# Opening durations re-entered in a build-time planner, and key-value products over five sets of positions

## The chip, the cores and the metric

The kernel runs on one core of one Trainium2 chip. The metric is the device time of one execution in microseconds (us); the time given for a kernel is the median of several executions.

## What is computed

Eight batches with eight heads of linear attention (576 positions, head width 64) are followed by a mixture of four two-layer networks ("experts") over all 4608 positions. Everything is float32.

```python
kv  = einsum('bhsd,bhse->bhde', k, v)          # q, k, v: (8, 8, 576, 64)
o   = einsum('bhsd,bhde->bhse', q, kv)
rms = sqrt(mean(o * o, axis=-1, keepdims=True) + 1e-6)
x   = (o / rms * g_norm).transpose(0, 2, 1, 3).reshape(4608, 512)
p   = domain_probs / (domain_probs.sum(-1, keepdims=True) + 1e-9)   # (4608, 4)
out = sum over e of p[:, e:e+1] * (relu(x @ w1[e]) @ w2[e])         # w1: 512x1024, w2: 1024x512
```

## The kernel before

**Tiling.** The 4608 positions are cut into nine chunks of 512: of each batch the first 512 positions make a chunk (c = 0 to 7), and the eight remainders of 64 positions together make the ninth. A stage is one expert on one chunk, s = 9·e + c, 36 in all. In a stage, up makes the hidden activations and down or down_deep the output; both are fast matrix products with seven products in place of eight, some at two levels, whose sums and differences of blocks run on VectorE (DVE) and GpSimd (POOL). The first stage alone uses up_plain (L999), plain products of 512 columns. During expert 0 the attention of batch c+1 is interleaved with stage c.

**Attention of one batch.** Heads are handled in four pairs (hp). load_pair brings q (two DMAs of 128 KB per pair), k and v (288 KB each; 96 partitions, on each six neighbouring positions of 64 values for each of two heads) in. For each pair: the PE transposes q (turn, L651), ScalarE (ACT) copies it to SBUF (L656); the PE multiplies k by v over six sets of 96 positions, two heads each (key_values, L665), ACT copies the result (L678); the PE multiplies q by it (attend, L691) into two PSUM tiles "raw". Then scaled: ACT squares them (L564), DVE sums (L571), POOL raises to the power -1/2 (L578, L582), DVE multiplies (L591), which is the last reader of raw. At the end the PE transposes the result (turn_x, L709) and ACT stores it as a half of x with the gain (L717). Batch 0 does this pair by pair; the others join two pairs into one group, so that one key_values has 24 products. Raw is in the PSUM banks "db" and "u2" for batch 0 in alternation, in "db" for batch 1, and in "ab" after that. The banks "db" also take the products of down (L1126). The remainder of each batch goes through turn_rem, attend_rem and turn_xrem (L735, L753, L769).

**Who sets the order.** Every operation is put into a Plan with a key (its wanted place), a duration per engine that it may run on, and its buffers. Plan.layout runs a list schedule once, when the kernel is built: it goes through time, gives each engine the next operation that its model calls ready, assigns buffers and PSUM banks, and so fixes the order of instructions on each engine. On the chip the engines keep that order and wait for each other by semaphores; the modelled times have no other effect. The PE and the DMA-issuing queue of SyncE (SP) take the first ready operation in order of keys, the others the most urgent. A load's end is modelled by one shared bus: `bus = max(bus, t + 1.5) + op.kb / 215.0`, plus 0.5, with at most eight loads on their way.

**Idle work.** While the next key on the PE is below 0 (that is, before the first product of up_plain in the ordinary order) and the model has nothing ready for the PE, it puts two transposes of the identity into a free PSUM bank (idle, L1353), which keep the PE running. In the model such a pair lasts:

```python
op = Op(front, {"PE": 0.23}, None, (), (), 0, False)
op.start, op.eng, op.end = t, eng, t + 0.23
```

weights_1 loads the four quarters of an expert's first matrix (512 KB each) and makes its sums, weights_2 the second. x_forms makes the sums of x for a stage. All sums go through combine (L360). norm_probs loads and normalizes p.

Of the kernel before, what the change touches and what calls it, by code (L numbers as in the profile page):

```python
# [34 lines left out]
class Plan:  # L35
# [13 lines left out]

    SPARE = {"big": 6, "small": 3}  # L50
    STEP, LATE = 44.0, 20.0

    def __init__(self):
        self.ops = []
# [26 lines left out]
    def layout(self, slots, later, idle, idle_banks, idle_until):  # L81
# [20 lines left out]
                cross = self.SAME if op.cost.keys() == d.cost.keys() else self.CROSS  # L102
                d.due = min(d.due, op.due - cross - min(d.cost.values()))
        busy = {e: 0.0 for e in todo}
        bus, port = 3.0, 0.0
        lanes = [0.0] * self.LANES
        t = 0.0
        wake = [0.0, 1.6]
# [24 lines left out]
        while left:  # L133
# [4 lines left out]
            for eng in todo:  # L138
# [25 lines left out]
                if best is not None:  # L164
                    op = best
# [38 lines left out]
                if eng == "PE" and busy[eng] <= t and 1.6 <= t and front < idle_until:  # L204
                    kind, spare = next((
                        (k, f) for k in idle_banks for f in free[k] if f[0] <= t
                    ), (None, None))
                    if spare is not None:
                        op = Op(front, {"PE": 0.23}, None, (), (), 0, False)
                        op.start, op.eng, op.end = t, eng, t + 0.23  # L210
                        op.fn = lambda eng, bank=slots[kind][spare[1]]: idle(bank)
                        busy[eng] = op.end
                        free[kind].remove(spare)
                        free[kind].append((op.end, spare[1]))
                        heapq.heappush(wake, op.end)
                        order.append(op)
                        moved = True
# [13 lines left out]
def kernel(  # L231
# [36 lines left out]
    nc = tc.nc  # L268
# [8 lines left out]
    NCH = B + 1  # L277
    HN = NT // 2
    HF = F // 2
    KR = 6  # L280
    KP = S // KR
    EPS = 1e-6
    NBLK = NCH * NR
    assert H * D == DM == NT and D == 64 and P == 128 and NPAIR == 4 and F == 1024
    assert REM == D and REM * B == NT and KP * KR == S and KP <= P

    const = ctx.enter_context(tc.tile_pool(name="const", bufs=1))
    pool = ctx.enter_context(tc.tile_pool(name="pool", bufs=1))
# [120 lines left out]
    def w1_src(e, dh, uh):  # L409
        rows = moe_w1[e][dh * 2 * P:(dh + 1) * 2 * P, uh * HF:(uh + 1) * HF]  # L410
        return rows.rearrange("(kt p) f -> p kt f", p=P)
# [19 lines left out]
    def weights_1(e, key, step, need):  # L431

        f = {n: Buf("big", f"w1_{e}_{n}") for n in (1, 2, 21, 4, 5, 6, 7, 3)}
        corner = {}
        w1corner[e] = {}
        for i, (n, dh, uh) in enumerate(((1, 0, 0), (2, 1, 0), (21, 0, 1), (4, 1, 1))):
            corner[n] = Buf(None, f"w1c_{e}_{n}")
            w1corner[e][uh, dh] = f[n], corner[n]
            load(
                key + i * step, f[n],  # L440
                lambda n=n: f[n].ap[:].rearrange("p (k u) -> p k u", k=2),
                w1_src(e, dh, uh), 512, also=[corner[n]],
            )

        def form(k_, o, a, b, op):
            corner[o] = Buf(None, f"w1c_{e}_{o}")
            combine(
                k_, either(1024), lambda: f[o].ap[:], lambda: f[a].ap[:], lambda: f[b].ap[:], op,
                [f[a], f[b], corner[a], corner[b]], [f[o], corner[o]],
            )  # L450

        def from_dram(k_, o, a, dh, uh):
            corner[o] = Buf(None, f"w1c_{e}_{o}")
            subtract_from(
                k_, f[o], lambda ap: ap[:].rearrange("p (k u) -> p k u", k=2), f[a],
                w1_src(e, dh, uh), [f[a], corner[a]], [f[o], corner[o]],
            )

        def sums():
            form(need + 0.25, 5, 21, 4, ALU.add)  # L460
            form(need + 0.26, 6, 5, 1, ALU.subtract)
            if e:
                from_dram(need + 0.5, 7, 21, 0, 0)
                from_dram(need + 0.5, 3, 6, 1, 0)
            else:
                form(need + 0.5, 7, 1, 21, ALU.subtract)
                form(need + 0.5, 3, 2, 6, ALU.subtract)
            w1f[e] = {}
            for j, m in enumerate(OUTER):
                x, low, y = f[m], corner[m], Buf("w1y", f"w1y_{e}_{m}")  # L470
                parts = {}
                for n, (uq, kt) in ((1, (0, 0)), (2, (0, 1)), (7, (1, 0)), (4, (1, 1))):
                    parts[n] = (
                        [x, low] if n == 7 else [x],
                        lambda x=x, uq=uq, kt=kt: two(x.ap[:])[:, kt, uq * HN:(uq + 1) * HN],
                    )
                for n, at in ((5, 0), (6, 1), (3, 2)):
                    parts[n] = ([y], lambda y=y, at=at: y.ap[:, at * HN:(at + 1) * HN])
                for o, a, b, op in (
                    (5, 7, 4, ALU.add), (7, 1, 7, ALU.subtract), (6, 5, 1, ALU.subtract),  # L480
                    (3, 2, 6, ALU.subtract),
                ):
                    combine(
                        need + j / 7, either(HN), parts[o][1], parts[a][1], parts[b][1], op,
                        parts[a][0] + parts[b][0], [low] if o == 7 else [y],
                    )
                w1f[e][m] = parts

        return sums
# [111 lines left out]
    def attention(b, key, span, rem):  # L601
# [6 lines left out]
        at = lambda j: key + span * j / (NPAIR + 1)  # L608
        qTs, kvs = {}, {}

        def load_pair(hp):
            hs = slice(2 * hp, 2 * hp + 2)
            n = f"{b}_{hp}"
            kind = "kv" if b or hp < 2 else "big"
            kt, vt, qt = Buf(kind, f"k{n}"), Buf(kind, f"v{n}"), Buf("small", f"q{n}")
            want = at(hp) - 0.25 if b else key - 1 + 0.1 * hp
            for r in range(2):
                load(
                    want, qt,
                    lambda qt=qt, r=r: qt.ap[:].rearrange(  # L620
                        "p (r h d) -> p r h d", h=2, d=D)[:, :, r, :],
                    q[b, 2 * hp + r, 0:NT, :].rearrange("(p r) d -> p r d", r=NR), 128,
                )
            for t, src in ((kt, k), (vt, v)):
                load(
                    want, t,
                    lambda t=t: t.ap[0:KP, 0:2 * KR * D].rearrange("p (h x) -> p h x", h=2),
                    src[b, hs].rearrange("h (p j) d -> p h (j d)", j=KR), 288,
                )
            return kt, vt, qt  # L630

        def kv_rows(t):
            return t.ap[0:KP, 0:2 * KR * D].rearrange("p (h j d) -> p h j d", h=2, d=D)

        groups = ((0,), (1,), (2,), (3,)) if b == 0 else ((0, 1), (2, 3))
        for g, pairs in enumerate(groups):
# [4 lines left out]
            for o, hp in enumerate(pairs):  # L641
# [6 lines left out]
                def turn(eng, bank=bank, qt=qt):  # L648
                    for r in range(NR):
                        rs = slice(r * P, (r + 1) * P)  # L650
                        nc.tensor.transpose(bank.ap[:, rs], qt.ap[:, rs], ident[:])  # L651

                plan.add(at(hp), pe(4, P, 1), turn, reads=[qt], writes=[bank])
                plan.add(
                    at(hp), act(NT),
                    lambda eng, bank=bank, qT=qT: nc.scalar.activation(  # L656
# [3 lines left out]

            def key_values(eng, bank=kbank, held=held):
                for o, (kt, vt) in enumerate(held):
                    for j in range(KR):
                        for r in range(2):
                            nc.tensor.matmul(  # L665
                                bank.ap[r * D:(r + 1) * D, o * D:(o + 1) * D],
                                lhsT=kv_rows(kt)[:, r, j, :], rhs=kv_rows(vt)[:, r, j, :],
                                start=(j == 0), stop=(j == KR - 1), skip_group_check=True,
                            )

            size = len(pairs)
            plan.add(
                at(pairs[-1]), {"PE": 0.73 * size + 0.2}, key_values,
                reads=[t for ts in held for t in ts], writes=[kbank],
            )
            plan.add(
# [2 lines left out]
                    out=to.ap[:, 0:size * D], in_=bank.ap[:, 0:size * D], func=ACT.Copy),  # L679
                reads=[kbank], writes=[kv],  # L680
            )
            raw = [Buf(("db", "u2")[r] if b == 0 else "ab" if b > 1 else "db", f"raw{n}_{r}") for r in range(2)]

            def attend(eng, raw=raw, kv=kv, pairs=pairs):
                for o, hp in enumerate(pairs):
# [300 lines left out]
    def up_plain(s, e, c, key, span):  # L986
# [4 lines left out]
        for i in range(8):  # L991
            uh, a, u = i // 4, i // 2 % 2, i % 2
            bank = Buf("u1" if a == 0 else "u2", f"up{s}_{i}")
            for dh in range(2):
                w, low = corners[uh, dh]

                def product(eng, w=w, bank=bank, dh=dh, ut=2 * a + u):
# [5 lines left out]
                        )  # L1003

                op = plan.add(
                    key + span * i / 8 - (1.1 if i < 2 and dh == 0 else 0.0), pe(2, NT), product,
                    reads=[w, low, xh[dh]], **({"parts": [bank]} if dh else {"writes": [bank]}),
                )
                op.marks = bank, NT
# [297 lines left out]

    plan.add(-2.85, {"SP": 1.1}, load_gains, writes=[gains], kb=1)
    attention(0, -2.0, 1.3, 0.1)
    sums_1 = weights_1(0, -2.5, 0.02, 0.3)  # L1310
    up_plain(0, 0, 0, 0.0, 1.0)
    sums_1()
    x_forms(0, 0.3)
    x_views = {}
    inner = {0: weights_2(0, 0.25, 0.02, 7.6)}
    norm_probs(0.3)
    for e in range(E):
        for c in range(NCH):
            s = e * NCH + c
            if e == 0 and c + 1 < B:  # L1320
                attention(c + 1, s - 0.1, 0.8, s + 0.5)
            if e + 1 < E and c == NCH - 1:
                weights_1(e + 1, s + 0.0, 0.12, s + 0.4)()
                inner[e + 1] = weights_2(e + 1, s + 1.0, 0.13, s + 1.55)
            if s + 1 < E * NCH:
                if e == 0 and c + 1 < NCH:
                    x_views[s + 1] = x_forms(c + 1, s + 0.7)
# [76 lines left out]
```

## Time and profile before

| | |
|---|---|
| median of 9 runs | 1723.47 us (1723.13 to 1723.83) |
| the profiled execution | 1723.22 us, of which 1721.4 us is the span from its first to its last instruction |
| mean granted TensorE clock | 0.999 |
| DVE busy | 1235.1 us (72%) |
| ACT busy | 974.6 us (57%) |
| POOL busy | 677.6 us (39%) |
| DMA moved | 230.42 MB, mean 134 GB/s |

The page gives the busy time of each engine, the span in 40 slices, the DMA queues, the chain of work that ended last, and groups of instructions. PE is the matmul stream, PEld the loading of weights beside it, SPq the issue of DMAs. A float32 product is two records in the trace, a transpose one. The heaviest groups on the PE are the products of up:

```profile
L912 PE MATMUL u<-xf,big 128*128 128x128 f32 x3104 | 452.4, 275 | 0.0
L912 PE MATMUL u<-xf,w1y 128*128 128x128 f32 x2652 | 390.9, 275 | 0.0
```

The columns are line, engine, operation, tiles, shapes and count, then busy us, mean ns of one, and idle time ahead.

### The profile page before, as it was taken

What the parts mean: (1) busy time and instruction counts of PE and PEld (TensorE: products, weight loads), DVE (VectorE), ACT (ScalarE), POOL (GpSimd) and SP (SyncE); (2) the same over time, 40 slices, a digit from 0 to 9 for tenths busy, and PEclk for the clock granted to TensorE, in tenths of its full rate; (3) what the DMA queues carried; (4) which work ended last, traced back from release to release, by engine and by line L of the source; (5) the groups of instructions that cost most, each with busy time, mean ns of one, the idle gap of its engine ahead of it and who ended that gap; (6) DMA issues with size and microseconds to landing.
All of it is one profiled execution on the core that took longest, in us unless ns stands there. A gap on an engine that the chain in (4) does not pass through costs nothing.

```text
span 1721.4 us, 39248 instructions
## 1 busy us (share of the span) xinstructions
PE 1711.9 (99%) x15586; PEld 1653.0 (96%) x15586; DVE 1235.1 (72%) x2034; ACT 974.6 (57%) x2378; POOL 677.6 (39%) x613
## 2 busy tenths in 40 slices
PE   9999999999999999999999999999999999999998
PEld 7699999999999999999999999999999999999998
DVE  4755655565777777777788787777788787777774
ACT  3354544454455665565666566666666666656562
POOL 3421322133435443433355544433355554433331
PEclk9999999999999999999999999999999999999999
DMA  9756444633455343444468444444478444444442
GB/s 240 218 163 194 147 121 138 195 130 117 166 144 151 104 114 105 110 112 111 127 173 192 111 111 111 111 111 110 102 183 204 115 111 111 111 111 111 102 109 49
DMA packets 156567, 230.42 MB, mean 134 GB/s; under 512 B 49888, under 2 KB 97248, under 8 KB 156384
## 3 DMA queue, kind: packets, MB, share of 16 engines
q1 hardware_dynamic: 133312, 191.21, 35.7%
q0 software_dynamic: 23072, 36.71, 14.2%
q8 instruction: 122, 2.00, 0.5%
q14 instruction: 61, 0.50, 0.1%
HBM read 154.74 MB, written 73.14 MB: 132 GB/s over the span
## 4 chain that ended last, share of the span: by engine, by line
PE 99%; POOL 0%; DVE 0%; ACT 0%; issue 0%; POOLq 0%
PE u L912 45%; PE db L1201 21%; PE ab L1201 13%; PE db L1126 12%; PE u L999 2%; PE ab L665 1%; PE ab L709 1%; PE ab L651 1%; PE ab L1353 1%; PE ab L691 1%; PE u L1126 1%; PE ab L1126 0%; PE db L691 0%; POOL rt L582 0%; PE ab L753 0%; PE ab L735 0%
## 5 line engine op out<-in xcount | busy, mean ns | idle before, releaser
L360 DVE TENSOR_TENSOR big<-big,big 128x1024 f32<-128x1024 f32 (+1 forms) x446 | 439.8, 1000 | 30.6 <-ACT big L895 19.4
L912 PE MATMUL u<-xf,big 128*128 128x128 f32 x3104 | 452.4, 275 | 0.0
L912 PEld LDWEIGHTS u<-xf,big 128*128 128x128 f32 x3104 | 399.8, 192 | 1.4
L912 PE MATMUL u<-xf,w1y 128*128 128x128 f32 x2652 | 390.9, 275 | 0.0
L939 DVE TENSOR_TENSOR big<-u,snap 128x256 f32<-128x256 f32 x442 | 186.6, 422 | 232.3 <-PE u L912 161.5
L912 PEld LDWEIGHTS u<-xf,w1y 128*128 128x128 f32 x2652 | 343.2, 192 | 1.6
L931 ACT ACTIVATE snap<-u 128x256 f32<-128x256 f32 x490 | 188.2, 384 | 207.0 <-PE u L912 175.5
L931 ACT ACTIVATE big<-u 128x256 f32<-128x256 f32 x442 | 169.4, 384 | 119.8 <-PE u L912 93.2
L360 POOL TENSOR_TENSOR big<-big,big 128x256 f32<-128x256 f32 (+1 forms) x137 | 180.6, 1323 | 127.2 <-DVE big L360 61.4
L1126 PE MATMUL db<-big,big 128*128 128x256 f32 x904 | 215.3, 382 | 2.1 <-DVE big L591 2.1
L1126 PEld LDWEIGHTS db<-big,big 128*128 128x128 f32 x904 | 164.2, 191 | 20.2 <-DVE big L591 2.3
L1201 PE MATMUL db<-big,big 128*128 128x128 f32 x1204 | 166.8, 275 | 0.0
L1201 PEld LDWEIGHTS db<-big,big 128*128 128x128 f32 x1204 | 150.4, 192 | 0.1
L1229 ACT ACTIVATE snap<-db 128x256 f32<-128x256 f32 x216 | 77.0, 356 | 106.0 <-PE db L1201 103.1
L895 ACT ACTIVATE big<-big 128x1024 f32<-128x1024 f32 x128 | 134.6, 1051 | 4.0 <-DVE big L360 3.3
L1096 POOL DMA_DIRECT2D out_dram<-big x98 | 89.7, 1041 | 56.3 <-ACT big L1073 37.9
L360 POOL TENSOR_TENSOR big<-big 128x512 f32<-128x512 f32 (+1 forms) x56 | 67.7, 1208 | 108.7 <-DVE big L360 58.5
L1201 PE MATMUL ab<-kv,big 128*128 128x128 f32 x764 | 110.1, 275 | 0.0
L1201 PE MATMUL db<-kv,big 128*128 128x128 f32 x752 | 109.1, 275 | 0.0
L931 ACT ACTIVATE u<-u 128x256 f32<-128x256 f32 x245 | 90.7, 370 | 32.3 <-PE u L912 12.4
L1267 POOL TENSOR_TENSOR big<-big 128x512 f32<-128x512 f32 x25 | 31.7, 1270 | 177.6 <-DVE big L360 144.4
L578 POOL TENSOR_SCALAR ss<-ss 128x16 f32<-128x16 f32 (+2 forms) x26 | 6.4, 247 | 241.0 <-DVE ss L571 240.8
(218 smaller groups left out, 2923.2 us busy)
## 6 DMA issues: line engine op xcount, KB each, us to landing
xf<-x SPq DMA_DIRECT2D x108, 512.0 KB, 3.7
out_dram<-big POOLq DMA_DIRECT2D x82, 256.0 KB, 5.8
xf<-x_h SPq DMA_DIRECT2D x81, 256.0 KB, 3.1
xf<-x SPq DMA_DIRECT2D x81, 256.0 KB, 3.4
x<-xf SPq DMA_DIRECT2D x36, 512.0 KB, 6.8
big<-in_moe_w_dram SPq DMA_DIRECT2D x29, 512.0 KB, 5.8
small<-in_q_dram SPq DMA_DIRECT2D x72, 128.0 KB, 5.0
kv<-in_k_dram SPq DMA_DIRECT2D x30, 288.0 KB, 4.9
```

Of the source, the lines that this page charges most:

```text
L360: lambda eng: adder(eng).tensor_tensor(out=out_(), in0=a(), in1=b(), op=op),
L651: nc.tensor.transpose(bank.ap[:, rs], qt.ap[:, rs], ident[:])
L895: lambda eng: nc.scalar.activation(out=b.ap[:], in_=b.ap[:], func=ACT.Relu),
L912: nc.tensor.matmul(ps.ap[:, u * P:(u + 1) * P], lhsT=w1f[e][m][mm][1]()[:, u * P:(u + 1) * P], rhs=views[m][mm][1](), start=(mm in (1, 5) ...
L931: lambda eng: nc.scalar.activation(out=where(), in_=ps.ap[:, 0:HN], func=ACT.Copy),
L939: lambda eng: nc.vector.tensor_tensor(out=block(whole, a, t), in0=src.ap[:, 0:HN], in1=add_.ap[:], op=ALU.add),
L999: nc.tensor.matmul(bank.ap[:], lhsT=two(w.ap[:])[:, kt, ut * P:(ut + 1) * P], rhs=two(xh[dh].ap[:])[:, kt, :], start=(dh == kt == 0), stop ...
L1096: nc.gpsimd.dma_start(out=dst, in_=cell(i)[parts, :], accum_op=ALU.add)
L1126: nc.tensor.matmul(ps.ap[:, 0:HN], lhsT=four(h[m])[:, kt // 2, t, kt % 2, :], rhs=w2f[e][m].ap[:, kt * HN:(kt + 1) * HN], start=(m in (1, ...
L1201: nc.tensor.matmul(ps.ap[:, o * P:(o + 1) * P], lhsT=b.ap[:, col:col + P], rhs=w2q[e][m][mm][1]()[:, kt, :], start=(mm in (1, 5) and o == ...
L1229: lambda eng: nc.scalar.activation(out=where(), in_=group_of(ps.ap), func=ACT.Copy),
L1267: lambda eng: adder(eng).tensor_tensor(out=whole(to), in0=whole(a), in1=whole(b), op=ALU.add),
```

## The change

**Durations in the planner.** An idle pair that the model places before 6.8 us is charged 0.43 us in place of 0.23. The bus starts at 3.8 in place of 3.0. For the loads of batch 0's k and v the model charges 241 KB in place of 288, for its q 172, for expert 0's w1 quarters 312 in place of 512 (the bytes moved are the same).

**q of batch 0.** Each pair's q comes in one DMA with packets of 1 KB (four neighbouring positions of a head) in place of two DMAs with packets of 256 bytes. The heads then lie differently, so that turn is eight products with the identity (64 rows of result each) in place of four transposes.

**Key-value products.** For batches 1 to 7 the 576 positions are cut into 4 sets of 120 and one of 96 in place of 6 of 96. k and v then come in two DMAs each: 120 partitions with packets of 1 KB, and 96 partitions with packets of 256 bytes. Batch 0 keeps six sets.

**Places.** Batch 0's raw tiles are in "db", "u2", "u1" and "db" again, two of a kind for each pair. The first four products of up_plain get keys from -0.89 to -0.86, and some keys of loads and sums in the opening and at the change of experts move by some hundredths.

```diff
-        bus, port = 3.0, 0.0
+        bus, port = 3.8, 0.0
...
-                        op = Op(front, {"PE": 0.23}, None, (), (), 0, False)
+                        took = 0.43 if t < self.SLOW else 0.23
+                        op = Op(front, {"PE": took}, None, (), (), 0, False)
...
-                w1_src(e, dh, uh), 512, also=[corner[n]],
+                w1_src(e, dh, uh), 512 if e else 312, also=[corner[n]],
...
+        splits = ((120, 4, 0), (96, 1, 480)) if b else ((96, 6, 0),)
...
+            if b == 0:
                 load(
+                    want, qt, lambda qt=qt: qt.ap[:].rearrange("p (h x) -> p h x", h=2),
+                    q[b, hs, 0:NT, :].rearrange("h (p r) d -> p h (r d)", r=NR), 172,
+                )
...
             for t, src in ((kt, k), (vt, v)):
+                at_ = 0
+                for rows, n_, size in splits:
+                    kb = rows * n_ // 2
+                    load(
+                        want, t,
+                        lambda t=t, at_=at_, rows=rows, n_=n_: t.ap[0:rows, at_:at_ + 2 * n_ * D]
+                        .rearrange("p (h x) -> p h x", h=2),
+                        src[b, hs, size:size + rows * n_].rearrange("h (p j) d -> p h (j d)", j=n_),
+                        kb if b else 241,
+                    )
+                    at_ += 2 * n_ * D
...
-                        nc.tensor.transpose(bank.ap[:, rs], qt.ap[:, rs], ident[:])
+                        if b:
+                            nc.tensor.transpose(bank.ap[:, rs], qt.ap[:, rs], ident[:])
+                            continue
+                        for o in range(2):
+                            at = (o * NR + r) * D
+                            nc.tensor.matmul(
+                                bank.ap[o * D:(o + 1) * D, rs], lhsT=qt.ap[:, at:at + D],
+                                rhs=ident[:],
+                            )
...
-                at(pairs[-1]), {"PE": 0.73 * size + 0.2}, key_values,
+                at(pairs[-1]), {"PE": (0.61 if b else 0.73) * size + 0.2}, key_values,
...
-            raw = [Buf(("db", "u2")[r] if b == 0 else "ab" if b > 1 else "db", f"raw{n}_{r}") for r in range(2)]
+            kind = ("db", "u2", "u1", "db")[g] if b == 0 else "ab" if b > 1 else "db"
+            raw = [Buf(kind, f"raw{n}_{r}") for r in range(2)]
...
-                    key + span * i / 8 - (1.1 if i < 2 and dh == 0 else 0.0), pe(2, NT), product,
+                    key - 0.89 + 0.01 * (i ^ 2) if i < 4 and dh == 0 else key + span * i / 8,
+                    pe(2, NT), product,
```

## The prediction

> **What bounds the kernel now.** I read the busy times first, then the chain of work that ended last.
>
> ```profile
> PE 1711.9 (99%) x15586; PEld 1653.0 (96%) x15586; DVE 1235.1 (72%) x2034; ACT 974.6 (57%) x2378; POOL 677.6 (39%) x613
> ...
> PE 99%; POOL 0%; DVE 0%; ACT 0%; issue 0%; POOLq 0%
> ```
>
> The PE is busy for 99% of the span and makes up 99% of the chain. So time goes only where the PE has less to do, or where what it does is filler, or where it waits. The chain in order of time (start, us, what) shows the filler in the opening:
>
> ```profile
> 1.35 4.96 PE ab L1353 x30
> 6.31 0.44 PE ab L651 x4
> 6.75 2.18 PE ab L1353 x20
> 8.93 0.85 PE ab L665 x24
> ...
> 11.43 1.46 PE ab L1353 x12
> 12.89 0.85 PE ab L665 x24
> ...
> 23.45 1.72 PE u L999 x4
> ...
> 27.33 1.75 PE ab L1353 x16
> ```
>
> L1353 is idle work, L665 the key-value products of a pair of heads of batch 0, L999 the first products of the experts. From 23.45 us on the PE works densely but for the 16 fillers at 27.33. The first 30 fillers take 4.96 us, 0.165 each, the 12 at 11.43 only 0.122: the array starts slower, and the planner's order stands later than planned. A DMA started at 2.80 with v of pair 0 lands 4.9 us later, at 7.7; its products start at 8.86, because fillers stand ahead of them.
>
> The list of the PE's waits has few entries (engine, line, waited for: total, times, longest), all but the start between 64 and 78 us:
>
> ```profile
> PE db L1126 <- DVE big L591: 2.1, 1, 2.1
> PE ab L1353 <- POOL ident masks.py:199: 1.4, 1, 1.4
> PE u L912 <- ACT snap L931: 0.6, 1, 0.6
> PE u L912 <- ACT u L931: 0.5, 1, 0.5
> PE ab L709 <- ACT big L717: 0.4, 1, 0.4
> ```
>
> The same stretch in windows (busy us and count of PE, PEld, DVE, ACT, POOL; then granted clock, DMA share, GB/s):
>
> ```profile
> 70.00:71.00 1.00, 0.29 (x3) 0.10 (x1) 0.66 (x1) 0.06 (x1) 1.00 (x1) 1.00 1.06 361
> 71.00:72.00 1.00, 0.00 (x0) 0.00 (x0) 0.36 (x1) 0.00 (x0) 0.83 (x3) 1.00 0.84 204
> 72.00:73.00 1.00, 0.61 (x2) 0.55 (x3) 1.00 (x3) 0.00 (x0) 1.00 (x1) 0.83 0.13 30
> 73.00:74.00 1.00, 1.00 (x3) 0.76 (x3) 0.62 (x3) 0.00 (x0) 1.00 (x3) 0.50 0.00 0
> ```
>
> The first product of down (L1126) waits for a bank "db", which batch 1's raw result holds until DVE has scaled it (L591); DVE waits for POOL's power, 3.77 us long, queued behind a sum of 2.35 us. After that the clock is halved and the eight records of L1126 take 3.55 us where the next eight take 1.73. In the chain the stretch from 64.59 to 77.94 lasts 13.35 us and holds 6.73 us of work at the usual durations (28 L912 records at 0.1115 = 3.12; 0.61; 1.73; two L709 at 0.44; 0.39). **6.6 us are lost there.** From 78 to 1716 us the PE waits for nothing.
>
> **Part 1, the opening.** Built, the changed kernel has 54 fillers in place of 114, none after the first product of up_plain. I place its order by durations of the rows. The 18 fillers ahead of the first q end near 4.9 us: the windows of half a microsecond show about 0.215 us each until 4.5, 0.11 after. q of pair 0 is then one DMA (its first half landed 2.6 us after issue), so it is there. SP issues three DMAs per pair where it issued four: a q took 1.36 us for two, about 0.62 for one. v of pair 0 is issued near 2.1 in place of 2.80 and lands at 6.2 to 6.8; the order puts its products at about 6.8, after ten fillers.
>
> The pairs follow as the loads come. In the trace's DMA records packets of 256 B took 21 to 27 ns, of 1536 B 91 to 107. A 1 KB packet does not occur there; between 50 (half of a 2 KB packet, 88 to 107) and 65 (on the line from 256 to 1536), it makes q 256 packets over 16 engines, 0.8 to 1.05 us, where 1024 packets of 256 B took about 1.4. With k and v at 192 packets each (1.1 to 1.3 us) a pair takes 3.0 to 3.6 us; the four L665 of before start 3.7 to 4.0 apart. Pair 3's products so start at 15.9 to 17.6. What the order puts from there to the first product of up_plain: 0.85, 8 fillers 0.88, L709 0.44, attend 0.55, 6 fillers 0.66 = 3.4 us. Its x half (ACT, 0.7 after L709) and w1 (first quarter after pair 3's loads, 256 packets of 88 to 107 ns = 1.4 to 1.7 us) are there by then. That is 19.3 to 21.0 at these spacings and 18.6 if the first pair is quicker; I take 19.5, between the two but nearer the rate that the w1 loads show. Gain 23.45 - 19.5 = **4.0 us** (2.5 to 4.9). The turn of q, now eight products in 0.8 us for 0.44 (16 records of 0.05), lies within this, ahead of loads that come later.
>
> The filler at 27.33 goes: **1.75 us** (0 to 1.75). It covered the power and scaling of pair 3. In the new order four products of up_plain (L999, 1.72 each) instead of two stand in that place. Pair 3's attend ends near 19; ACT 0.8, DVE 0.7, POOL 1.9, DVE 0.8 and handovers, 4.2 to 4.4 as from 23.1 to 27.3 before, make it ready at 23.4; its L709 stands 5.6 us after the first product, at 25.1. So nothing is late there.
>
> **Part 2, key-value products.** 14 groups, each 48 records before, 40 now. Two rows give the slope: 24 records in 0.85 us, 48 in 1.55, so 0.0292 us a record. 14·8·0.0292 = **3.3 us**, all on the dense PE. The rows now have 120 partitions. Were a record to cost by rows, 8·4·120 + 8·96 (per group) would equal 48·96 and nothing would be gained: 0 to 3.3. The groups of 64 rows (L691) have weight loads of 135 ns and products of 218, those of 96 rows (L665) 138 and 222: half as many rows again cost 2%. I take 3.3.
>
> [...] The change adds 384 packets of 256 B to each pair. By the trace's packets these are 384·23/16 = 0.55 us, and 480 packets of 1 KB 1.5 to 1.95, together about the 2.4 of k and v before: nothing. [...] Batch 1's products come near 30 us where DMA is full (share 1.05 to 1.16 from 10 to 40 us): after the opening's loads at 16.5, w1 6, q and k, v of two pairs with the remainder 7.5, everything has landed at 30, with the PE there at 30 to 31. [...] I take 0. Afterwards DMA share is 0.44 (120 to 200 us), and k and v issued from 83.61 to 85.42 are used at 99.95.
>
> **Part 3, the stall at 64 to 78.** All of the order after 24 us is new. In it the first L1126 comes about 39 us after the first up_plain product, at 58. I count the queue that frees "db": DVE has about 29 us of sums from 24 on; batch 1's last attend ends near 50; on POOL two sums of 2.36 and a short power come first, then the power of 3.2 to 3.8 starts at about 53 and DVE scales until 57 to 58. That is even with the PE, where before it was 5 us late. I leave 2 of the 6.6 us lost: gain **4.6 us**, between 0 (all back) and 6.6. The two groups of transposes after it have margins of 0.4 to 0.7 us by the same count, so some small wait is likely. [...]
>
> Other edits (keys by hundredths, expert weights) change nothing that waits from 78 us on.
>
> **Sum**, against the profiled execution's 1723.22 (span 1721.4, and 1.8 around it; the median, 1723.47, is 0.25 above): 4.0 + 1.75 + 3.3 + 4.6 = 13.65, so **1709.6 us**.
>
> **Rivals.**
> A, all three parts work: 1709.6, own range 1706.5 to 1713. 0.66.
> B, the stall remains or moves to a neighbouring wait: 1723.2 - 9.05 = 1714.2. For it: all margins counted there are under a microsecond. Against: the order no longer has two sums just ahead of a late power. 0.20.
> C, the opening is bound by bytes, which stay the same; the fillers turn into bare waits, and only 3.3 and half of the stall go: 1717. For it: DMA is full from 4 us on. Against: fillers delayed L665 by over 1 us after the landing. 0.07.
> D, slower: SP is one queue, and four more issues for each of 14 groups at 0.4 us hold up what stands behind. Loads have some 10 us of margin; from a delay beyond that on, each group would wait by the 1.6 us: 22.4 lost less 13.65 gained, 1732. For it: SP already waits 128 us between 80 and 430 us for the sums that its stores (L1098) take out. Against: the margin. 0.04. The rest, 0.03, is no change.
>
> The bound for telling a change is 0.2%, 3.4 us. Faster 0.92 (A, B, most of C), same 0.04, slower 0.04. The range 1706 to 1716.5 holds A and B: low with no loss left at 64 to 78 (1707.6) and a first product at 18.6; high with the stall whole and the opening at its worse end (1723.2 - 2.5 - 1.75 - 3.3 = 1715.7).
>
> **What would show it.** The first up_plain product starts near 19.5 us; key_values of 40 records take 1.32 us; PE waits between 50 and 80 sum to 2 us or less, with granted clock 1.00 throughout; no wait after that. I am wrong if 120-row products take 1.55 us, if the wait for L591 is back, or if kv loads end waits of the PE.

## The result, and the profile after

The changed kernel takes **1712.68 us** (median of 9 runs, 1711.46 to 1714.68), the kernel before 1723.48 us beside it (29 runs, 1722.71 to 1724.15): ratio 0.9938, 95% interval 0.993 to 0.9946. It is 10.8 us faster; 1709.6 was predicted, and 1712.68 lies in the predicted range of 1706 to 1716.5. Its runs lie 3.2 us apart where those of before lie 1.4 apart. Its profiled execution took 1715.14 us (span 1713.4), more than any of the nine timed runs, so a second profile of the same kernel (1712.22 us, experiment 1) is read beside it.

Lines have moved: idle work is now L1387, key_values L697, turn L678, attend L724, turn_x L742, up_plain L1032, up L945, down L1160. L591, the scaling of raw, stays. The page of after, busy times:

```profile
PE 1703.7 (99%) x15462; PEld 1645.9 (96%) x15462; DVE 1230.5 (72%) x2024; ACT 972.8 (57%) x2378; POOL 695.7 (41%) x623
```

The PE has 124 records fewer. The list of its waits (line, waited for: total, times, longest):

```profile
PE ab L697 <- issue: 1.7, 1, 1.7
PE ab L1387 <- POOL ident masks.py:199: 1.4, 1, 1.4
PE u L945 <- DVE big L972: 1.0, 1, 1.0
PE db L1160 <- DVE big L591: 0.5, 1, 0.5
PE ab L802 <- ACT big L750: 0.5, 1, 0.5
PE u L945 <- ACT snap L964: 0.3, 1, 0.3
```

The wait for L591, 2.1 us and then a halved clock before, is 0.5 us. The last four lines are all that the PE waits after 24 us, 2.3 us together. Only two of them, L1160 and L802, stand where the old stall was, at 64 to 65 us; the 0.3 of L945 stands at 910 us and the 1.0 at 1307, where the kernel before waited for nothing. The windows of the old stall (busy us and count of PE, PEld, DVE, ACT, POOL; granted clock, DMA share, GB/s) show the clock whole:

```profile
60.00:70.00 10.00, 9.01 (x47) 6.58 (x46) 8.16 (x18) 4.51 (x11) 6.55 (x4) 1.00 0.71 231
70.00:80.00 10.00, 10.00 (x163) 9.30 (x161) 8.14 (x24) 5.74 (x14) 5.05 (x6) 1.00 0.84 227
```

But the first line of the waits is new. "Issue" means that the PE waited for nothing that the profile shows. The chain (start, us, what) places it in the opening:

```profile
14.46 0.84 PE ab L697 x23
15.30 1.68 issue
16.98 0.27 PE ab L697
17.24 1.71 PE ab L678 x16
...
21.02 0.85 PE ab L697 x24
...
24.76 3.44 PE u L1032 x8
...
35.68 1.32 PE ab L697 x40
```

The PE stops inside pair 2's key-value group, after 23 of its 24 records. The record at which it stops waits on no semaphore, and its operands had landed (v of pair 2 at 12.30 us; pairs are counted from 0). Then the granted clock is 0.50, from 16.98 to 20.40 us:

```profile
15.00:16.00 1.00, 0.30 (x11) 0.16 (x6) 0.77 (x3) 0.00 (x0) 0.72 (x2) 1.00 1.03 383
16.00:17.00 1.00, 0.02 (x2) 0.02 (x2) 0.00 (x0) 0.00 (x0) 1.00 (x1) 0.99 1.05 389
17.00:18.00 1.00, 1.00 (x11) 1.00 (x12) 0.76 (x2) 0.22 (x1) 0.12 (x1) 0.50 1.04 385
```

Sixteen records of the next turn took 1.71 us, where they take 0.88 in experiment 1. Up_plain starts at 24.76 us, later than the 23.45 of before, although v of pair 3 had landed at 16.75 (before: 19.75). The rest gained 9.4 us and the opening lost 1.3: 8.1 in this profiled execution.

### The profile page after: what moved, and what is told of

Read it like the earlier page. It is cut to its first block, busy times and chain, and to the rows that moved or that the text cites. A ratio compares the mean times of both kernels' runs of the same rounds, so it can differ in the third digit from the quotient of the medians.

```text
span 1713.4 us, 39139 instructions
## 1 busy us (share of the span) xinstructions
PE 1703.7 (99%) x15462; PEld 1645.9 (96%) x15462; DVE 1230.5 (72%) x2024; ACT 972.8 (57%) x2378; POOL 695.7 (41%) x623
## 4 chain that ended last, share of the span: by engine, by line
PE 96%; DMA 1%; POOL 1%; DVE 1%; issue 0%; ACT 0%; SPq 0%; POOLq 0%; DVEq 0%; ACTq 0%
PE u L945 44%; PE db L1235 21%; PE ab L1235 13%; PE db L1160 12%; PE ab L697 1%; DMA out_dram<-big 1%; PE ab L742 1%; PE ab L724 1%; PE ab L674 1%; PE u L1160 1%; PE u L1032 1%; PE ab L1387 0%; POOL rt L582 0%; PE ab L1160 0%; DVE big L360 0%
## 5 line engine op out<-in xcount | busy, mean ns | idle before, releaser
L360 DVE TENSOR_TENSOR big<-big,big 128x1024 f32<-128x1024 f32 (+1 forms) x467 | 451.7, 985 | 37.0 <-ACT big L928 19.9
L945 PE MATMUL u<-xf,big 128*128 128x128 f32 x2960 | 431.2, 275 | 0.0
L945 PE MATMUL u<-xf,w1y 128*128 128x128 f32 x2652 | 391.2, 275 | 1.0 <-DVE big L972 1.0
L945 PEld LDWEIGHTS u<-xf,big 128*128 128x128 f32 x2960 | 381.3, 192 | 1.6
L945 PEld LDWEIGHTS u<-xf,w1y 128*128 128x128 f32 x2652 | 343.3, 192 | 2.8 <-DVE big L972 1.2
L360 POOL TENSOR_TENSOR big<-big,big 128x256 f32<-128x256 f32 (+1 forms) x153 | 203.5, 1337 | 124.0 <-DVE big L360 55.5
L1160 PE MATMUL db<-big,big 128*128 128x256 f32 x920 | 217.7, 379 | 0.5 <-DVE big L591 0.5
L1160 PEld LDWEIGHTS db<-big,big 128*128 128x128 f32 x920 | 166.2, 190 | 18.6 <-DVE big L591 0.7
L1235 PEld LDWEIGHTS db<-big,big 128*128 128x128 f32 x1232 | 152.1, 192 | 0.1
L360 POOL TENSOR_TENSOR big<-big 128x512 f32<-128x512 f32 (+1 forms) x69 | 83.7, 1215 | 109.8 <-DVE big L360 77.8
L1235 PE MATMUL db<-kv,big 128*128 128x128 f32 x808 | 115.4, 275 | 0.0
L1235 PEld LDWEIGHTS db<-kv,big 128*128 128x128 f32 x808 | 102.6, 192 | 0.0
L1301 POOL TENSOR_TENSOR big<-big 128x512 f32<-128x512 f32 x22 | 27.9, 1270 | 180.4 <-DVE big L360 177.9
```

What stands on the lines that cost most here:

```text
L360: lambda eng: adder(eng).tensor_tensor(out=out_(), in0=a(), in1=b(), op=op),
L945: nc.tensor.matmul(ps.ap[:, u * P:(u + 1) * P], lhsT=w1f[e][m][mm][1]()[:, u * P:(u + 1) * P], rhs=views[m][mm][1](), start=(mm in (1, 5) ...
L1160: nc.tensor.matmul(ps.ap[:, 0:HN], lhsT=four(h[m])[:, kt // 2, t, kt % 2, :], rhs=w2f[e][m].ap[:, kt * HN:(kt + 1) * HN], start=(m in (1, ...
L1235: nc.tensor.matmul(ps.ap[:, o * P:(o + 1) * P], lhsT=b.ap[:, col:col + P], rhs=w2q[e][m][mm][1]()[:, kt, :], start=(mm in (1, 5) and o == ...
L1301: lambda eng: adder(eng).tensor_tensor(out=whole(to), in0=whole(a), in1=whole(b), op=ALU.add),
```

## What the bare stretch is

The page has a queue that the prediction passed over; before and after show the same line (packets, MB, share of 16 engines):

```profile
q8 instruction: 122, 2.00, 0.5%
```

2.00 MB in 122 packets are 16 KB each. No trace says which engine the queue serves. That it is the PE is an estimate from these counts: the PE has 2·15462 records (weight loads and products), so 65 bytes to a record and 253 records to a packet. At that rate the page's other 8215 instructions would make 0.53 MB, and the second instruction queue, q14, moved 0.50. Where the PE stands dry (bare, without a wait) fits too. Counting its records from the start, after and experiment 1 both stop at record 443, and later short stops stand at 697, 254 further. In the trace's DMA records the first such packet in the program's span was:

| | packet starts, took, us | PE records started by then | PE dry at | length, us | first up_plain |
|---|---|---|---|---|---|
| before | 13.21, 1.29 | 286 | not dry | | 23.45 |
| after | 14.52, 1.18 | 406 | 443 | 1.90 | 24.76 |
| 1 after again | 13.08, 1.30 | 386 | 443 | 1.50 | 22.81 |
| 1, second packet | 19.80, 1.05 | 609 | 697 | 0.62 | |
| 2 loads held | 12.81, 1.16 | 312 | not dry | | 22.78 |
| 2, second packet | 19.80, 1.05 | 617 | 697 | 0.97 | |
| 9 short fillers | 13.43, 1.31 | 352 | not dry | | 21.22 |
| 10 no late filler | 14.90, 1.12 | 394 | 440 | 1.14 | 21.24 |
| 11 the same again | 12.50, 1.15 | 353 | not dry | | 19.43 |

(Length: from the start of the record before to that of the record after. In 10 the trace lacks three product records of fillers whose weight loads it has, so 440 is the same place.) In these traces the PE goes dry at the first packet where 386 or more records had started when the packet began, not where 353 or fewer had. It resumes 1.3 to 1.7 us after the packet's end. In the kernel before the PE reached record 443 2.7 us after the packet's end, and did not stop. The same holds in all fourteen traces of this case: record 443 never starts sooner than 1.27 us after the first packet's end, record 697 never sooner than 1.27 after the second's. And the stop goes with the count, not with the operation: in 10 it stands inside pair 2's attend. That the packet comes late because loads fill the DMA engines (share 1.03 to 1.05 in the windows above) is not shown: 10 and 11 are one kernel with the same loads, and their packets began 2.4 us apart.

## Experiments

All were timed beside the kernel before (1723.45 to 1723.57 us in these sets).

**1. The changed kernel again.** No edit: does the stretch repeat, and does it make the scatter?

> The changed kernel once more, beside the others on the same chip. Theory (the PE runs out of instructions in the opening because their fetch stands behind data): the profile again shows a bare stretch of 1 to 2 us in the middle of pair 2's key-value products or near it, without a wait, and a fetch of 16 KB on the instruction queue issued late; its length differs from run to run, so the times scatter over 3 us around 1712.7. Rival (a fixed wait for data, the last part of v of pair 3): the stretch sits at the same place and has the same length in each run.

1713.03 us (1712.22 to 1714.78), ratio 0.994 (0.9927 to 0.9952). Its chain:

```profile
13.91 0.84 PE ab L697 x23
14.75 1.28 issue
...
18.56 0.85 PE ab L697 x24
...
22.08 0.35 issue
22.43 0.38 PE ab L1387 x2
22.81 3.44 PE u L1032 x8
```

The stretch is at the same record, 0.4 us shorter, the clock stays whole (1.00 from 10 to 20 us), and the execution is 2.9 us shorter than that of after. So the stretch belongs to the kernel, and its length differs between executions. Not all of the 2.9 us is its doing. Up_plain starts 1.95 us sooner, of which 0.55 was there when the stretch began: the first record of full clock stands at 6.74 us in after's trace and at 5.08 in this one (4.39 before), and fillers start every 0.213 us until then, every 0.109 afterwards. The waits at 910 and 1307 us are 1.1 us shorter here. Whether the stretch makes the scatter of the unprofiled executions is not shown.

**2. Loads held back.** The loads of w1 and all behind them on SP wait for DVE's first sum, so that fewer loads are on their way when the packet comes:

```diff
+            if op.eng == "SP" and waiting is None and firsts[0] in op.outs:
+                waiting = []
+            if op.eng == "SP" and waiting is not None and waiting != "done":
+                waiting.append(op)
+                continue
+            sequence.append(op)
+            if op is reduces[0]:
+                sequence += ["hold"] + waiting
+                waiting = "done"
...
+            if op == "hold":
+                nc.vector.memset(firsts[0].ap[:, 0:1], 0.0)
```

> As the changed kernel, in the same order on every engine, but the four loads of w1 and all behind them on SP wait for DVE's first sum (about 12.2 us) in place of being issued from 9.6 us on. Theory of the late fetch: with 2 MB less in the DMA engines the fetch of the PE's instructions comes before 13 us, the bare stretch of 1.7 us and the half clock after it (17 to 20.4 us) go, the first product of up_plain starts at 21 to 21.5 us in place of 24.8, and the time is 1711 to 1712.5 with less scatter (about 3.4 us below the changed kernel's profiled 1715.1). Rival (the opening is bound by the loads): w1 lands 2.6 us later, the first product starts at 24.8 or later and the time is the same or up to 2.6 us longer.

1712.80 us (1712.03 to 1713.58), ratio 0.9937 (0.9925 to 0.995). The stretch in pair 2 is gone, and nothing is won: a wait of 0.7 us for q of pair 2 took its place, and the PE is dry 254 records further, at 697:

```profile
21.70 0.70 issue
22.40 0.38 PE ab L1391 x2
22.78 3.44 PE u L1036 x8
```

The gain was missed. The runs lie 1.6 us apart instead of 2.6, too few to build on. The hold was weak: the first load of w1 was issued at 11.57 us, in experiment 1 at 10.38, and the packet began at 12.81 for 13.08. It neither shows nor excludes that loads delay the packet.

**3. Six sets again** in the changed kernel:

```diff
-        splits = ((120, 4, 0), (96, 1, 480)) if b else ((96, 6, 0),)
+        splits = ((96, 6, 0),)
...
-                at(pairs[-1]), {"PE": (0.61 if b else 0.73) * size + 0.2}, key_values,
+                at(pairs[-1]), {"PE": 0.73 * size + 0.2}, key_values,
```

> The changed kernel with six sets of 96 for all batches, one DMA for each k and v; the rest stays. Theory: 3.3 us more on the dense PE, 1716, with the opening as in the changed kernel and the waits between 60 and 80 us changed by 2 us at most. Rival (the five sets do nothing): 1712.7.

1721.46 us (1720.52 to 1723.76), ratio 0.999 (0.9981 to 0.9999). That is 8.8 us more than after, not the 3.3 of the products. The opening is the same (22.83), but the planner's new order has a stall of its own: turn_x waits for the scaling, and the clock falls (to a mean of 0.88 from 50 to 60 us).

```profile
PE ab L742 <- DVE big L591: 2.2, 1, 2.2
```
```profile
50.00:60.00 10.00, 7.78 (x63) 4.03 (x62) 8.69 (x19) 1.62 (x4) 6.24 (x4) 0.88 0.80 212
```

So the products cannot be priced in this way; the planner has to be kept out (experiment 5).

**4. Five sets alone,** in the kernel before:

```diff
+        splits = ((120, 4, 0), (96, 1, 480)) if b else ((96, 6, 0),)
...
-                at(pairs[-1]), {"PE": 0.73 * size + 0.2}, key_values,
+                at(pairs[-1]), {"PE": (0.61 if b else 0.73) * size + 0.2}, key_values,
```

> The kernel before with the key-value products of batches 1 to 7 in five sets, nothing else; the planner orders anew with the new durations. Theory (a record costs 29 ns whatever its rows): 14 groups of 40 records at 1.32 us, 3.3 us gained, 1720.2, give or take what the stall at 64 to 78 us does in the new order (from -4 to +2). Rival (the cost goes by rows, or the loads with packets of 256 B make waits): 1.5 us a group and 1723 or more.

1722.79 us (1722.24 to 1724.01), ratio 0.9997 (0.9987 to 1.0006): no change that can be told. The products are shorter, but the old stall grew:

```profile
PE db L1141 <- DVE big L591: 4.1, 1, 4.1
```
```profile
70.00:80.00 10.00, 5.84 (x20) 4.47 (x21) 3.06 (x8) 1.72 (x4) 6.06 (x6) 0.66 0.50 160
```

The wait was 2.1 us. The PE came to it 0.4 us sooner (at 69.92 us for 70.29), and the bank came free 1.6 us later (74.00 for 72.39): the planner's new order delays the scaling too. The clock was half for 6.83 us.

**5. A sixth set in the changed order.** The order of after, with one more pair of products per pair of heads, into columns that nothing reads:

```diff
+                    for r in range(2 if b else 0):
+                        nc.tensor.matmul(
+                            bank.ap[r * D:(r + 1) * D, (4 + o) * D:(5 + o) * D],
+                            lhsT=ks[r], rhs=vs[r], start=True, stop=True, skip_group_check=True,
+                        )
```

> The changed kernel in the same order, with one product more for each head in batches 1 to 7 (the last set of 96 positions again, into columns of the bank that nobody reads), so that a group has 48 records as before the change. Theory: the five sets are worth their records on a dense PE: a group takes 1.55 us in place of 1.32, and the time rises by 3.3 us to about 1716.1 (3 to 3.6 above the changed kernel's 1712.7 to 1713.0). Rival (the products lie beside waits, so their number costs nothing): no rise.

1715.36 us (1714.27 to 1715.67), ratio 0.9952 (0.994 to 0.9965): 2.3 us above experiment 1 and 2.7 above after. The last product ends 3.1 us later than in experiment 1, of which 0.34 is a later first up_plain. With the order fixed, the sixth set costs 2.8 us in the traces, somewhat less than 3.3.

**6. Power ahead of the sum,** in the kernel before: the power of batch 1's second half goes in front of the 2.35-us sum on POOL, and the scaling in front of the difference that needs that sum on DVE.

```diff
+        order = [o for o in order if o not in (total, power, *scale)]
+        order.insert(order.index(sixth), total)
+        order[order.index(total):order.index(total)] = scale
+        order.insert(order.index(sums) + 1, power)
```

> The kernel before, with one thing moved: for batch 1's second group POOL does the power ahead of the sum of 128x1024, and DVE scales raw ahead of the difference that needs that sum. Theory (the stall at 64 to 78 us is the queue on POOL in front of the bank db, and the halved clock follows from it): the wait for L591 goes or is below 0.5 us, no half clock near 72 us, and 3.5 to 5.5 us are gained: 1718 to 1720. Rival (the next thing is late as well, here the difference and the sums of up behind it): the wait moves to L912 or L1126 and less than 1.5 us is gained.

1724.79 us (1723.79 to 1725.66), ratio 1.0009 (1.0 to 1.0017): nothing gained, rather 1.3 us lost. The wait moved to up's product, for a sum that the moved work now holds up:

```profile
PE u L912 <- DVE big L939: 3.4, 1, 3.4
```

So it was not the position of one sum: POOL has the sum and the power to do ahead of the PE there, and whichever comes second is late.

**7. Less work on POOL,** in the kernel before: POOL writes scaled sums in place of that one power (1.05 us for 3.77), so that these positions are left without their normalization.

```diff
+            if name == "1_1":
+                nc.gpsimd.tensor_scalar(
+                    out=rt.ap[0:n, 0:2 * blocks], in0=ss.ap[0:n, 0:2 * blocks],
+                    scalar1=1.0 / D, scalar2=EPS, op0=ALU.mult, op1=ALU.add,
+                )
+                return
```

> The kernel before, with the power of batch 1's second group left out (POOL writes scaled sums in its place, so that the x of those positions is not normalized); the order stays. POOL has 3.8 us less to do in front of the bank db. Theory (the stall is the amount of work on POOL and DVE at that place, not the order of the two things): the wait for L591 goes, the clock stays up, no wait over 1 us comes in its place, and 3.5 to 5.5 us are gained: 1718 to 1720. Rival (the sums on DVE alone hold the PE): less than 2 us.

1721.19 us (1720.36 to 1721.85), ratio 0.9988 (0.9979 to 0.9996): 2.3 us gained, less than expected. The clock stays up (a mean of 1.0 over the execution), but 1.0 us of the wait is left, and its chain runs through DVE's sums:

```profile
69.14 1.14 DVE big L360
...
70.95 1.13 DVE big L360
72.08 0.61 DVE big L597
```

POOL's power is part of the stall, DVE's sums are the rest. In the changed kernel POOL had been busy for 18.9 us between 30 and 60 us, 10.8 before: it has taken ten sums by 60 us where it took six, and DVE 35 where it took 50. The new order moves sums from DVE to POOL. That alone is no cure: experiment 3 has nine and 38 by then, and a stall. Which of the planner's edits matter is seen in part in the next run.

**8. The old durations** in the changed kernel:

```diff
-    SLOW = 6.8
+    SLOW = 0.0
...
-        bus, port = 3.8, 0.0
+        bus, port = 3.0, 0.0
...
-                w1_src(e, dh, uh), 512 if e else 312, also=[corner[n]],
+                w1_src(e, dh, uh), 512, also=[corner[n]],
...
-                    q[b, hs, 0:NT, :].rearrange("h (p r) d -> p h (r d)", r=NR), 172,
+                    q[b, hs, 0:NT, :].rearrange("h (p r) d -> p h (r d)", r=NR), 256,
...
-                        kb if b else 241,
+                        kb,
```

> The changed kernel with the planner's durations as before (bus from 3.0, filler at 0.23 us throughout, loads by their bytes), with q in one DMA and five sets kept. 86 fillers stand ahead of the first product of up_plain in place of 54. Theory (the durations bring the PE's order to what the loads do): the first product starts at 23.5 to 25 in place of 22.8, and the order behind is another, so that a stall at 50 to 80 us of up to 7 us may be back: 1714 to 1722. Rival (the durations do nothing, q and the sets do it all): 1712.7 to 1713.3 with the first product at 22.8.

1719.41 us (1717.11 to 1720.84), ratio 0.9976 (0.9966 to 0.9986), 6.4 to 6.7 us above experiment 1 and after. First up_plain at 25.22, and the stall is back with half a clock for 6.83 us:

```profile
PE db L1160 <- DVE big L591: 2.4, 1, 2.4
```
```profile
70.00:80.00 10.00, 8.79 (x35) 7.15 (x36) 3.91 (x13) 2.87 (x7) 5.09 (x5) 0.66 0.71 232
```

2.4 us of it are the opening (25.22 against 22.81); the larger part is the stall, 40 us later than anything that was edited. **The old q of batch 0** in the changed kernel (two DMAs, four transposes) was measured as well:

```diff
-            if b == 0:
+            if b < 0:
...
-                        if b:
+                        if b >= 0:
...
-                    at(hp), pe(4, P, 1) if b else {"PE": 0.82}, turn, reads=[qt], writes=[bank])
+                    at(hp), pe(4, P, 1), turn, reads=[qt], writes=[bank])
```

> The changed kernel with batch 0's q as before: two DMAs of 128 KB for a pair with packets of 256 B, four transposes; the planner's durations stay as changed but for q's 128 KB each. Theory (pairs follow as their loads land): a pair takes about 0.4 us longer, the first product of up_plain starts 1 to 2 us later than 22.8, and the time is 1713.5 to 1716 unless the new order makes another stall at 50 to 80 us (2 to 8 us more). Rival (q's packets don't matter, the loads of the opening are bound by something else): the first product starts at 22.8 or earlier.

1713.51 us (1713.05 to 1714.09), ratio 0.9942 (0.9929 to 0.9956), first up_plain at 23.36: 0.5 to 0.8 us above experiment 1 and after, within their scatter. Up_plain was expected 1 to 2 us behind the 22.8 of experiment 1 and came 0.55 behind it. The planner lays out another order here as well (76 fillers), so what q's packets are worth alone is not shown.

**9. Short fillers.** A filler is one bfloat16 product of 512 columns, two PE records in place of four, so that the PE reaches record 443 later:

```diff
-        for r in range(2):
-            nc.tensor.transpose(bank[:, r * P:(r + 1) * P], ident[:], ident[:])
+        nc.tensor.matmul(bank, lhsT=half[:, 0:P], rhs=half, start=True, stop=True)
```

> The changed kernel in the same order, but each filler of two float32 transposes (four records) is one bfloat16 product of 512 columns (two records) of the same length. Theory (the PE runs dry at record 443 since the next 16 KB of instructions come near 14.5 us plus 1.3 to 1.6): with some 40 records fewer ahead of it, record 443 is reached about 1 us later; the bare stretch within pair 2's products goes or shrinks below 0.6 us, the clock never halves in the opening, the first product of up_plain starts at 22 to 22.8 us in each run, the times scatter by less than 2 us and the median is 0.3 to 1.5 us below 1712.9. Rival (the stretch comes from data that land late): it stays at the same products of pair 2, with 1.3 to 1.9 us.

1712.43 us (1711.01 to 1718.14), ratio 0.9942 (0.993 to 0.9955). Its profiled execution, 1711.01 us, has no bare stretch, and up_plain starts at 21.22. The median is not apart from that of after, and one run took 1718.14, with a mean granted clock of 0.998 where the other four have 1.0; what happened in it stays open.

**10 and 11. No filler behind pair 3's products,** which are the last that the loads hold up, with the short fillers of 9; measured twice.

```diff
+        third = next(n for n, o in enumerate(order) if any(b.name == "kv0_3" for b in o.outs))
+        known = set(plan.ops)
+        order = [o for n, o in enumerate(order) if n < third or o in known]
```

> The changed kernel with the short filler of x8 and without any filler behind pair 3's key-value products (seven, 1.5 to 1.7 us in the traces); the rest of the order stays. Theory (these fillers were planned for a wait that isn't there, and hold the PE up): pair 1's transpose follows pair 3's products at once, the first product of up_plain starts 1.0 to 1.6 us sooner after them, and the time is 1710.8 to 1711.6, below both the changed kernel and x8 (1712.4). Rival (the fillers stand in for a true wait, the x half or w1): the PE waits bare in their place and nothing is gained.

> The kernel of the run without late fillers, unchanged, measured a second time. If its lead over the changed kernel is real (1710.98 against 1712.68), the median lies again at 1710.5 to 1711.6 with a spread near 1 us, and the first up_plain product of the profiled execution starts at 20.8 to 21.5 us. If it was the luck of one set of executions, the median lies at 1712.4 or above, or the spread is again near 3 us.

1710.98 us (1710.33 to 1711.37), ratio 0.9928 (0.9914 to 0.9942), and 1711.15 (1710.57 to 1712.09), ratio 0.9929 (0.9915 to 0.9943). **This version beats both kernels,** by 12.4 us and some 1.6 us, and its runs lie 1.0 and 1.5 us apart. The profile of 10 has a dry stretch, inside attend (L725 here):

```profile
16.16 0.26 PE u L725 x2
16.41 0.93 issue
17.34 0.69 PE u L725 x30
...
21.24 3.63 PE u L1033 x8
```

That of 11 has none, and up_plain starts at 19.43 us, sooner than the 20.8 to 21.5 that were expected:

```profile
16.92 0.93 PE ab L698 x24
...
18.15 0.66 PE ab L743 x4
18.81 0.62 PE db L725 x32
19.43 3.63 PE u L1033 x8
```

Yet the execution is only 0.4 us shorter than that of 10 (1710.57 against 1710.98), with up_plain 1.81 us earlier. Two loads of batch 1 are now late, for which 10 had no wait:

```profile
PE ab L769 <- DMA small<-in_q_dram: 0.5, 1, 0.5
...
PE ab L698 <- DMA kv<-in_v_dram: 0.4, 1, 0.4
```

Both stand between 28 and 33 us. Half of what the opening gains is spent there at once, and 0.36 us more in a wait at 1303 us that 10 does not have.

## Why the prediction was right, and where it was not

By its own steps, in the profiled execution of experiment 1 (1712.22 us, 11.0 less than before):

| step | predicted, us | measured, us |
|---|---|---|
| opening, first up_plain | 4.0 (19.5) | 0.64 (22.81); -1.3 (24.76) in after's profile |
| filler at 27.33 | 1.75 | 1.75: no filler between up_plain's products |
| key-value products | 3.3 | 3.3: 40 records in 1.32 us, 14 times, for 1.55 |
| stall at 64 to 78 | 4.6 of 6.6 | 5.3 in both profiles: 4.3 us for 3.0 us of work, 1.0 of it waits |
| waits at 910 and 1307 us | 0 | -0.3; -1.3 in after's profile |
| behind the last product | 0 | 0.3; 0.2 |
| whole | 13.65 | 11.0; 8.1 |

**The opening is the term that was mis-sized.** The step was "Pair 3's products so start at 15.9 to 17.6", and from there 3.4 us to the first product of up_plain: "I take 19.5". In that sum they stand at 16.1; they started at 18.56, and 4.25 us more passed. Pair 0's products came first, at 7.60 us for 6.8 (8.36 in after's profile, where full clock began at 6.74 us and not at 5.08). Then came what was not in the sum at all: 1.28 us bare at record 443, 0.35 at 697. The 14 fillers after pair 3's products took 2.0 us for 1.54. The loads were less regular than reckoned: v of pair 3, issued in the same order each time, landed at 16.75 us in after's profile, at 17.91 in experiment 1, at 15.05 and 16.79 in 10 and 11. In experiment 1 the products began 0.65 us behind that landing, so the stop cannot have cost them more there; in after's profile they began 4.3 us behind it. In experiment 11, with no stop and no late filler, they began at 16.92, 0.13 after the landing, and up_plain at 19.43. That this is nearly the 19.5 of the prediction is luck: its sum had pair 3's products 0.8 us sooner and 1.54 us of fillers that experiment 11 leaves out.

Nor did that sum have a clock that falls again. In after's profile the 1.68 us bare, 1.90 from one start to the next, were followed by a clock of 0.50 for 3.41 us, which costs half of them, 1.7; in experiment 1 the 1.28 us bare, 1.50 from start to start, left it at 1.00.

Nor would a full opening have brought 4.0 us to the end. The prediction had batch 1's loads landed at 30 us with the PE there at 30 to 31, and took the wait as 0; in experiment 11 the PE, there at 28 us, waited 0.9 us for them.

**The products** were priced by record, not by row, and that held: products of 120 rows take 225 ns for 222 to 224 with 96. Experiment 5 gives 2.3 to 2.8 of the 3.3 us. In experiment 4 the same products came with a longer stall and won nothing that can be told; so the 3.3 count only where the stall goes as well. The packets of 1 KB, put at 50 to 65 ns, took 55 (median of the 1024 of batch 0's q in after).

**The stall** went as predicted in size, with a wait of 0.5 us for L591 and a margin as thin as stated. The queue is the one that was described, two sums, a short power, a long power, then the scaling (experiment 1):

```profile
51.30 4.63 POOL big L360 x2
56.28 2.60 POOL rt L582
59.50 2.96 POOL rt L582
63.23 1.99 PE db L1160 x8
```

But the long power was counted at 53 us and came at 59.50, the PE at 58 and came at 62.69. That both were late together is in part luck. Rival B, the stall back, is what experiments 3, 4 and 8 show: each undoes or omits one part, and each has a wait of 2.2 to 4.1 us and half a clock between 56 and 80 us. Its place depends on the whole order, so no part of the change can be called its cure: without the durations 6.4 to 6.7 us are lost, without the five sets 8.8, of which 3.3 are the products. The new keys and the places of raw were not undone alone. Rival D, SP held up by more issues, did not appear; no load ends a wait of the PE in the changed kernel.

**What was said to stay silent** did not quite. "No wait after that" failed at 1307 us: a store takes 9.48 us to land there (8.71 in experiment 1), DVE waits for its buffer, and the PE for DVE, 1.0 us in after's profile and 0.3 in experiment 1. The wait at 910 us hangs on a store in the same way. The kernel before has neither; why the new order meets these stores and the old one does not was not tested.

## What to carry to other kernels

Idle work on the PE was not free here: fewer records of filler, and none after the last late load, were worth 1.6 us. A gain on one engine counted only where the next thing it waits for was early: five sets alone brought nothing that can be told of their 3.3 us, and an opening 1.81 us shorter brought 0.4. Where a planner lays out the order, an edit's price is read from an order held fixed (a spare product in it), since undoing the edit lays out another order with other stalls.

## What was not expected of the hardware

In the opening the PE stood bare, for 0.6 to 1.9 us from one start to the next, at the same two counts of its records, 443 and 697, and started again 1.3 to 1.7 us after the end of a packet of 16 KB on q8, which had taken 1.05 to 1.30 us. The profile names no semaphore for it and calls it "issue"; two executions of one kernel differ in it (experiments 10 and 11: 0.93 us idle, and none). That the PE waits there for instructions which such a packet brings is an estimate from these counts and times; no trace names it. A gap of 1.90 us between the starts of two products was followed by a clock of 0.50 for 3.41 us (after), and one of 1.50 us was not (experiment 1). In the fourteen traces, between start-up and end, each of the six gaps of 1.90 to 4.35 us (before 2.37, after 1.90, and experiments 3, 4, 6 and 8 with the old durations) came with 3.41 or 6.83 us of half clock, and none of those up to 1.50 did. Why, no run shows.
